# Local attention values in four row tiles of the transposed weights, constant products at the start, and a new order: attention and a two-layer product on one core

## The chip, the cores and the metric

The kernel runs on one core of a Trainium2 chip. The metric is the device time of one execution in microseconds (us). Five engines matter: TensorE (PE) multiplies matrices, VectorE (DVE), ScalarE (ACT) and GpSimd (POOL) work on elements, SyncE (SP) issues the transfers (DMA). Each engine takes its instructions in the order of its own list and waits on semaphores for the others.

## The reference

Eight batches of eight heads, 576 positions, 64 values per head. Two attentions are added: a global one on means of four positions, repeated four times, and a local one in which a position sees those less than four away. The sum, laid out as 4608 rows of 512, goes through a two-layer product with a squared ReLU.

```python
out_d = sm_attn(q_d, k_d, v_d)                     # on means of 4 positions: 144 x 144
out_up = np.repeat(out_d, factor, axis=2)
mask = np.abs(pos[:, None] - pos[None, :]) < factor
scores = scale * np.matmul(q, k.transpose(0, 1, 3, 2))
scores = np.where(mask, scores, -1000000000.0)
...
out_local = np.matmul(attn, v)
return (out_up + out_local).astype(np.float32)

h = x @ w_in                                       # 4608 x 512 by 512 x 2048
r = np.maximum(h, 0.0)
g = s * (r * r) + b
return (g @ w_out).astype(np.float32)
```

## The kernel before, in words

A unit is one batch and one pair of heads; there are 32, numbered 4 × batch + pair. The 128 partitions hold 2 heads × 64 values where a product runs over the values of a head.

Batches 0 to 2 (units 0 to 11) do the local attention on PE, in `banded`. A row of 576 positions is cut into 24 windows of 24 positions; a window needs 32 keys. `near` (tokens `l0` to `l11`) computes for each head the products of q and k window by window (tile sl, L416 to L421: a mask through a 16-bit product, then 24 small products in column tiles), takes the maximum and the difference on DVE (L431, L432), the exponential on ACT (L436), the sum and its reciprocal on DVE (L438 to L440), and normalises (L442), on POOL for batch 0 and on DVE for the others. DVE's 32×32 transpose (L449) turns the weights to keys × positions (tile pt). ACT then copies each of four 32-row blocks onto the diagonal of a 128×128 block for each group of four windows (tile db, L453); everything off the diagonal was set to zero at the start. A product of 128 rows of v (vw) with 96 columns of that block gives four windows at once (tile ol, L464), twice per unit, a half each, and DVE adds the half to the global part (ups) into x (L468). The global part of a unit is `far` (tokens `d0` to `d11`): `down` reduces q and k (L308, L310), multiplies (sa, L327), takes the softmax on DVE and ACT, transposes on PE, and multiplies with the means of v, which `values` (tokens `v0` to `v11`) adds up on POOL.

Batches 3 to 7 do the local part on POOL and DVE instead, in `local_unit` (tiles lqk, pr, st, pv, acc), and only the global part on PE. Their first block of q and k uses the buffer `big`, which before holds db of unit 0 as well.

Weights come as 64-bit numbers and are converted in 22 chunks (tokens `c0` to `c21`, `convert`): ACT L252, DVE L254 to L258, ACT L260, DVE L262. Both layers use pairs of high and low parts: three products each. `x` is split by `begin_x` and its like (xh on ACT, xl on DVE, L747). For a block t of 256 rows and an eighth p of the inner width the upper products are L617 (tile ph, token `G`, two for each t and p), ReLU, square and the high part are ACT's L630 to L632 (`R`), the low part is DVE's L637 (`V`), and the lower products are L691 to L693 (tile po, `H`). The row sums of the second weights, for the constant b, are added up on DVE (L650, L653, token `b`) and multiplied by ones on PE (cs, L658, token `s`); only then can the first blocks be written out (`evict`, L669).

What sets the order: for everything up to the 28th pair (t, p), the text PLAN. Each word is one step of the generator with that name; `wNi`, `wNo` and `qN` issue loads. `in_order` ties the instructions of PE, DVE, ACT and POOL to that order, engine by engine, and `tc.high_priority` puts all of it ahead of the rest. Behind it the code runs by `advance`, the same before and after.

Before the plan run the clears (L789 to L792): DVE sets dq and the blocks of unit 3 and unit 0 to zero, ACT copies zeros into those of units 1 and 2 (L218).

Of the kernel before, what the change touches and what calls it, by code (L numbers as in the profile page):

```python
# [11 lines left out]
F32 = mybir.dt.float32  # L12
F32R = mybir.dt.float32r
I32 = mybir.dt.int32
BF16 = mybir.dt.bfloat16
# [36 lines left out]
HF = 7  # L52
GROUPS = [(i // HP, i % HP // 2) for i in range(EU, B * HP, 2)]
# [33 lines left out]
def attention_ffn_kernel(ctx, tc, qk, vw_in, vr_in, vdm, qkn, vn, w_in, w_out, s_in, b_in, out):  # L87
# [65 lines left out]

    ident = cst.tile([P, P], F32, name="ident")
# [45 lines left out]
    db = one.tile([P, 2 * NG, P], F32, tag="big", name="db")  # L200

# [5 lines left out]
    diag = {0: (db, *blocks(dq, 0, dq[:, QV:]))}  # L207
# [3 lines left out]
    def clear(i):  # L211
        da, vm = room[i]["dg"], room[i]["sc"][:, 1536:1792]
        n = 2 * NG * P
        for part in (da[:, n : n + QV], vm, da[:, 0:n]):
            if i == 3:
                nc.vector.memset(part, 0.0)
            else:
                nc.scalar.copy(part, zero.to_broadcast([P, part.shape[1]]))  # L218
        diag[i] = (take(da, 0, [P, 2 * NG, P]), *blocks(da, n, vm))
# [66 lines left out]
    def add_values(b, hp, tmp, dg):  # L286

        _, _, vdr, vm = dg
# [685 lines left out]
```

## Time and profile before

| | us |
|---|---|
| median of 3 runs | 957.62 (956.99 to 958.03) |
| profiled execution | 957.84 |
| its span | 956.0 |

How to read the profile: times are those of one execution on the core. A row of a timeline has its start in the span, its length, the engine, the line, the operation, out<-in with their shapes, how many were merged, and in brackets how long the engine was idle before it and what ended that. A row of the stretches has the stretch, its length, then the busy time and count of PE, of PE's weight loads, of DVE, ACT and POOL, the granted clock of PE, the busy share of DMA and its rate. A row of waits says who waited for whom, how long in all, how often, and the longest. The records of fp32 products are two for each instruction.

The early part by slices of a fortieth of the span (23.9 us each); each digit is the busy share in tenths:

```profile
PE   6699999999999999999999999999999999999998
DVE  8999999845587788787868787887777321112021
ACT  7977774466552636344454544454544333333231
PEclk9699999999999999999999999999999999999999
```

### The profile page before, as it was taken

The numbers are of one execution on the slowest core, as the hardware profiler recorded it, in microseconds if no ns is written. First come the engines' busy times: TensorE is split into PE (matmuls) and PEld (weight loads), VectorE is DVE, ScalarE is ACT, GpSimd is POOL, SyncE is SP. The second block draws the span as 40 slices with busy tenths as digits, with TensorE's granted clock in tenths as the row PEclk, the third lists the DMA queues.
The fourth block names the chain that finished last, engine by engine and source line by source line (L and its number), as shares of the span: only waits on it lengthen the run. The fifth ranks groups of instructions, "written<-read, shape, count | busy, mean of one in ns | idle before, by whom it ended". The sixth has DMA issues, their size and how long they took to land.

```text
span 956.0 us, 18449 instructions
## 1 busy us (share of the span) xinstructions
PE 928.4 (97%) x7316; PEld 835.7 (87%) x7316; DVE 639.5 (67%) x1134; ACT 476.8 (50%) x1133; POOL 416.2 (44%) x440
## 2 busy tenths in 40 slices
PE   6699999999999999999999999999999999999998
PEld 5588888888898999998899999999899999999986
DVE  8999999845587788787868787887777321112021
ACT  7977774466552636344454544454544333333231
POOL 6401130010577676867776868676776200000000
PEclk9699999999999999999999999999999999999999
DMA  9755413123232323323232323232311000000000
GB/s 322 268 167 183 143 46 118 63 75 100 87 117 89 117 90 110 95 80 108 88 116 80 126 80 126 81 126 79 114 55 44 1 23 2 23 1 23 1 23 22
DMA packets 31750, 86.25 MB, mean 90 GB/s; under 512 B 3248, under 2 KB 7856, under 8 KB 31664
## 3 DMA queue, kind: packets, MB, share of 16 engines
q1 hardware_dynamic: 31664, 85.08, 26.9%
q8 instruction: 57, 0.93, 0.4%
q14 instruction: 29, 0.24, 0.1%
HBM read 75.63 MB, written 9.44 MB: 89 GB/s over the span
## 4 chain that ended last, share of the span: by engine, by line
PE 84%; DVE 7%; DMA 3%; POOL 2%; ACT 1%; issue 1%; SPq 0%; DVEq 0%; POOLq 0%
PE ph L617 38%; PE po L691 13%; PE po L692 13%; PE po L693 12%; PE sa L327 2%; PE ol L464 1%; PE up L368 1%; POOL pr L522 1%; DMA tqk<-in_qk_dram 1%; PE ot L554 1%; DMA wst<-in_moe_w_in_dram 1%; DMA tvd<-in_vdm_dram 1%; PE up L366 1%; PE sl L421 1%; DVE es L257 1%
## 5 line engine op out<-in xcount | busy, mean ns | idle before, releaser
L617 PE MATMUL ph<-xh,wi 128*128 128x256 f32 x2176 | 406.7, 280 | 1.5 <-DVE gl L637 1.5
L617 PEld LDWEIGHTS ph<-xh,wi 128*128 128x128 f32 x2176 | 342.0, 189 | 7.3 <-DVE gl L637 1.9
L617 PE MATMUL ph<-xl,wi 128*128 128x256 f32 x1152 | 323.4, 281 | 0.0
L522 POOL TENSOR_TENSOR pr<-lqk 128x576 f32<-128x576 f32 x140 | 201.3, 1461 | 77.7 <-DMA lqk<-in_qkn_dram 47.7
L617 PEld LDWEIGHTS ph<-xl,wi 128*128 128x128 f32 x1152 | 217.3, 189 | 4.5
L630 ACT ACTIVATE ph<-ph 128x512 f32<-128x512 f32 x144 | 83.7, 582 | 248.1 <-PE ph L617 239.4
L691 PE MATMUL po<-wo,gh 128*128 128x512 f32 x456 | 181.8, 399 | 2.0 <-DVE os L669 1.7
L693 PE MATMUL po<-wo,gl 128*128 128x512 f32 x456 | 179.1, 394 | 1.1 <-DVE gl L637 1.0
L692 PE MATMUL po<-wo,gh 128*128 128x512 f32 x456 | 180.2, 395 | 0.0
L637 DVE TENSOR_TENSOR gl<-ph,gh 128x512 fp32r<-128x512 f32 x114 | 77.9, 684 | 125.0 <-ACT gh L632 124.7
L544 POOL TENSOR_TENSOR acc<-acc,pv 128x576 f32<-128x576 f32 x80 | 121.0, 1512 | 48.8 <-DVE acc L544 25.9
L524 DVE TENSOR_REDUCE st<-pr 128x9 f32<-128x576 f32 x140 | 105.9, 757 | 31.7 <-POOL pr L522 28.2
L693 PEld LDWEIGHTS po<-wo,gl 128*128 128x128 f32 x456 | 85.7, 188 | 20.5 <-DVE gl L637 2.5
L691 PEld LDWEIGHTS po<-wo,gh 128*128 128x128 f32 x456 | 85.7, 188 | 18.7 <-DVE os L669 2.1
L632 ACT CAST gh<-ph 128x512 fp32r<-128x512 f32 x114 | 66.6, 586 | 66.4 <-PE po L692 61.1
L692 PEld LDWEIGHTS po<-wo,gh 128*128 128x128 f32 x456 | 85.8, 188 | 15.7 <-DVE wo L262 0.3
L297 POOL TENSOR_TENSOR dq<-vt 80x64 f32<-80x64 f32 x58 | 22.6, 401 | 174.5 <-PE up L368 172.9
L543 DVE TENSOR_TENSOR pv<-lv,st 128x576 f32<-128x576 f32 x120 | 86.9, 747 | 14.2 <-POOL acc L544 13.6
L631 ACT ACTIVATE ph<-ph 128x512 f32<-128x512 f32 x144 | 83.8, 583 | 3.5
L692 PE MATMUL po<-wo,gb 128*128 128x512 f32 x120 | 47.8, 398 | 0.0
L691 PE MATMUL po<-wo,gb 128*128 128x512 f32 x120 | 47.1, 392 | 0.0
L693 PE MATMUL po<-wo,gb 128*128 128x512 f32 x120 | 46.8, 392 | 0.0
(158 smaller groups left out, 1167.5 us busy)
## 6 DMA issues: line engine op xcount, KB each, us to landing
tqk<-in_qk_dram SPq DMA_DIRECT2D x30, 584.0 KB, 3.9
lqk<-in_qkn_dram SPq DMA_DIRECT2D x20, 768.0 KB, 4.6
lv<-in_vn_dram SPq DMA_DIRECT2D x20, 480.0 KB, 3.4
out_dram<-os SPq DMA_DIRECT2D x17, 512.0 KB, 3.0
wst<-in_moe_w_in_dram SPq DMA_DIRECT2D x7, 1024.0 KB, 6.2
wst<-in_moe_w_out_dram SPq DMA_DIRECT2D x7, 1024.0 KB, 5.0
tvd<-in_vdm_dram SPq DMA_DIRECT2D x29, 160.0 KB, 2.6
tvr<-in_vr_dram SPq DMA_DIRECT2D x29, 128.0 KB, 3.1
```

The source lines that it names most:

```text
L522: nc.gpsimd.tensor_tensor(pr, lqk[:, 0:CH], lqk[:, CH + o : 2 * CH + o], ALU.mult)
L524: nc.vector.tensor_reduce(ls[:, :, o], pr, AX.X, ALU.add)
L543: nc.vector.tensor_tensor(pv, lv[:, o : o + CH], w, ALU.mult)
L544: (nc.vector if o % 3 == 1 else nc.gpsimd).tensor_tensor(acc[:, :, h], acc[:, :, h], pv, ALU.add)
L617: nc.tensor.matmul(ph[:, j], wi[p][:, s, k, f], xk[:, k], start=k == 0 and s == 0 and xk is xh, stop=k == NK - 1 and s == 1)
L630: nc.scalar.activation(ph, ph, AF.Relu)
L631: nc.scalar.activation(ph, ph, AF.Square)
L632: nc.scalar.copy(gh, ph)
L637: nc.vector.tensor_tensor(gl, acc.pop((t, p)), gh.bitcast(F32), ALU.subtract)
L691: nc.tensor.matmul(po[m], gh[:, j, ms], wo[p][:, 0, j], start=first, stop=False)
L692: nc.tensor.matmul(po[m], gh[:, j, ms], wo[p][:, 1, j], start=False, stop=False)
L693: nc.tensor.matmul(po[m], gl[:, j, ms], wo[p][:, 0, j], start=False, stop=last)
```

## The change

**The local products.** The copies onto a diagonal go, and with them the tile db, its zeros and the part of the clears that made them. Each window is now a product of its own: 32 rows of v, by row tile of the window (tile position 32·w), with 24 columns of pt, into 64 partitions by head (column tile 64·h). A half f takes windows w = 2f and 2f + 1 of each group into two banks, ol0 and ol1, so a half is 24 products (before: 6) and two additions of 144 positions (before: one of 288), whose target is 6 pieces of 24 positions, 96 apart.

**Constant products.** DVE sets a 16-bit tile warm to one, and PE multiplies it with itself 14 times, 512 columns each, into a bank that nobody reads, ahead of q's first products.

**Normalising.** The multiplication runs on POOL for batches 0 and 1, on DVE for batch 2.

**The order.** PLAN is new throughout.

```diff
+WARM = 14
 PLAN = (
-    "d0 d0 l1 d1 l0 l1 d1 d2 d1 d3 d2 l1 d1 d3 d0 v1 l1 l0 l1 d1 l1 l0 d0 d1 l1 l2 d1 l0 d0 "
+    "d0 l0 d0 d1 l1 d0 l1 d1 l2 d0 d1 d2 d0 l0 d2 d1 l0 l2 d1 d2 l0 v2 l1 d3 d1 l2 l3 l2 d3 "
...
+    warm = two.tile([P, 4 * TB], BF16, tag="gh", name="warm")
+    nc.vector.memset(warm, 1.0)
+    spare = bank(7, [P, DM], "spare")
+    for _ in range(WARM):
+        nc.tensor.matmul(spare, warm[:, 0:P], warm[:, 0:DM], start=True, stop=True)
...
-    db = one.tile([P, 2 * NG, P], F32, tag="big", name="db")
...
-        n = 2 * NG * P
-        for part in (da[:, n : n + QV], vm, da[:, 0:n]):
+        for part in (da[:, 0:QV], vm):
...
-            (nc.vector if b else nc.gpsimd).tensor_tensor(
+            (nc.vector if b > 1 else nc.gpsimd).tensor_tensor(
...
-            for w in range(4):
-                ws = slice(32 * w, 32 * w + 32)
-                nc.scalar.copy(bd[ws, :, ws], pt[ws])
-            yield
...
             for f in range(2):
-                n = S // 2 // FAC
-                ol = banks([P, S // 2], "ol")
-                for gg in range(NG // 2):
-                    g = f * (NG // 2) + gg
-                    for h in range(2):
-                        hs = slice(64 * h, 64 * h + 64)
-                        pw = bd[:, h * NG + g, :].rearrange("p (w c) -> p w c", w=4)
-                        nc.tensor.matmul(
-                            ol[hs, 96 * gg : 96 * gg + 96], vw[:, g, hs], pw[:, :, 0:TW],
-                            start=True, stop=True)
+                ol = [banks([P, NG, TW], f"ol{i}") for i in range(2)]
+                for g in range(NG):
+                    for i in range(2):
+                        w = 2 * f + i
+                        ws = slice(32 * w, 32 * w + 32)
+                        for h in range(2):
+                            hs = slice(64 * h, 64 * h + 64)
+                            nc.tensor.matmul(
+                                ol[i][hs, g], vw[ws, g, hs], pt[ws, h * NG + g, 0:TW],
+                                start=True, stop=True, tile_position=(32 * w, 64 * h))
                 yield
-                nc.vector.tensor_tensor(
...
+                uv = ups.rearrange("p (g w s) -> p w g s", g=NG, w=4)
+                for i in range(2):
+                    w = 2 * f + i
+                    nc.vector.tensor_tensor(
+                        xv[:, w], ol[i].rearrange("p g (s j) -> p g s j", j=FAC),
+                        uv[:, w].unsqueeze(3).to_broadcast([P, NG, TW // FAC, FAC]), ALU.add)
...
-            nc.vector.memset(db, 0.0)
```

Lines behind the first edits shift by a few: what was L308, L421, L431, L442 and L449 is L311, L423, L433, L444 and L451 in the changed kernel; the new local products are L463, the new additions L470, the constant's memset and products L155 and L158. L617 to L693 keep their numbers.

Three places in the built order. First, DVE's start, before (dq and db are zeroed blocks, flat a buffer of units 1 to 3, tqk q and k of a unit, sl q's products):

```order
L216 MEMSET flat_80 128x416
L216 MEMSET flat_79 128x256
L216 MEMSET flat_80 128x1536
L792 MEMSET db_145 128x1536
L174 CAST idb_133<-ident_96 128x128
L308 TENSOR_REDUCE qd_200<-tqk_67 128x144
L310 TENSOR_REDUCE kd_201<-tqk_67 128x144
L176 CAST maskb_135<-mask_101 128x128
L177 CAST maskb_135<-mask_101 128x2x32
L308 TENSOR_REDUCE flat_69<-tqk_72 128x144
L310 TENSOR_REDUCE flat_69<-tqk_72 128x144
L431 TENSOR_REDUCE flat_71<-sl0_206 128x6
```

Both lists begin behind the memset of dq (L789), which stays. DVE's start in the changed kernel:

```order
L219 MEMSET flat_80 128x416
L219 MEMSET flat_79 128x256
L155 MEMSET warm_96 128x1024
L180 CAST idb_150<-ident_113 128x128
L311 TENSOR_REDUCE qd_212<-tqk_67 128x144
L313 TENSOR_REDUCE kd_213<-tqk_67 128x144
L182 CAST maskb_152<-mask_118 128x128
L183 CAST maskb_152<-mask_118 128x2x32
L311 TENSOR_REDUCE flat_69<-tqk_72 128x144
L313 TENSOR_REDUCE flat_69<-tqk_72 128x144
L433 TENSOR_REDUCE flat_71<-sl0_246 128x6
```

The two memsets of 1,536 are gone, the constant's stands in their place, and the first reduction of sl now reads the second of PE's sets (sl0_246) instead of the first.

Second, PE's start, before:

```order
L416 LDWEIGHTS idb_133
L416 MATMUL sl0_206<-maskb_135,idb_133 128x192
L421 MATMUL sl0_206<-tqk_72 32x32 x24
L416 LDWEIGHTS idb_133
L416 MATMUL sl0_234<-maskb_135,idb_133 128x192
L421 MATMUL sl0_234<-tqk_67 32x32 x24
L327 MATMUL sa_266<-flat_69,flat_70 96x144 x3
```

And in the changed kernel, from the last of the 14 constant products on:

```order
L158 LDWEIGHTS warm_96
L158 MATMUL spare_98<-warm_96 128x512
L418 LDWEIGHTS idb_150
L418 MATMUL sl0_216<-maskb_152,idb_150 128x192
L423 MATMUL sl0_216<-tqk_67 32x32 x24
L418 LDWEIGHTS idb_150
L418 MATMUL sl0_246<-maskb_152,idb_150 128x192
L423 MATMUL sl0_246<-tqk_72 32x32 x24
L330 MATMUL sa_275<-kd_213,dq_156 96x144 x3
```

The constant's products stand ahead of q's, and unit 0's set now comes before unit 1's.

Third, DVE at the weights of unit 4, the first of batch 1, before (pl are the weights, sm their sums, es, wi and wo weights of the two-layer product in conversion):

```order
L440 RECIPROCAL sm_818<-sm_818 128x12
L254 TENSOR_SCALAR es_869<-es_869 128x1024
L255 TENSOR_SCALAR es_869<-es_869 128x1024
L637 TENSOR_TENSOR gl_961<-ph_905,gh_960 128x512
L257 SCALAR_TENSOR_TENSOR es_822<-wst_159,es_822 128x512
L258 SCALAR_TENSOR_TENSOR es_822<-wst_159,es_822 128x512
L262 TENSOR_TENSOR wi_851<-es_853,wi_851 128x1024
L442 TENSOR_TENSOR pl_817<-pl_817,sm_818 128x384
L257 SCALAR_TENSOR_TENSOR es_869<-wst_665,es_869 128x1024
L258 SCALAR_TENSOR_TENSOR es_869<-wst_665,es_869 128x1024
L449 STREAM_TRANSPOSE pt_1091<-pl_817 128x384
```

And in the changed kernel:

```order
L442 RECIPROCAL sm_960<-sm_960 128x12
L260 SCALAR_TENSOR_TENSOR es_1077<-wst_175,es_1077 128x512
L261 SCALAR_TENSOR_TENSOR es_1077<-wst_175,es_1077 128x512
L451 STREAM_TRANSPOSE pt_1146<-pl_959 128x384
L433 TENSOR_REDUCE sm_1155<-sl0_1102 128x6
```

The multiplication between reciprocal and transpose has left DVE's list (it is L444 in POOL's now); two conversions of 512 stand between the two. Elsewhere in PE's list, 210 lower products (L691 to L693) stood ahead of the column sums L658 and 216 do now, while 456 upper products (L617) stand ahead of them in both. On the DMA queue the first block of the later batches (lqk) now comes ahead of batch 1's first q.

More of the change, by code (lines that the diff above doesn't have):

```diff
@@ L205, in blocks @@
                 take(vm, 0, [KM, 2, P]))
-    diag = {0: (db, *blocks(dq, 0, dq[:, QV:]))}
+    diag = {0: blocks(dq, 0, dq[:, QV:])}
     zero = dq[:, QV - 1 : QV]
@@ L218, in clear @@
                 nc.scalar.copy(part, zero.to_broadcast([P, part.shape[1]]))
-        diag[i] = (take(da, 0, [P, 2 * NG, P]), *blocks(da, n, vm))
+        diag[i] = blocks(da, 0, vm)
     wi, wo, wst = {}, {}, {}
@@ L286, in add_values @@
     def add_values(b, hp, tmp, dg):
-        _, _, vdr, vm = dg
+        _, vdr, vm = dg
         tvr, tvd = ld[(b, hp)]["vr"], ld[(b, hp)]["vd"]
@@ L300, in down @@
     def down(b, hp, banks, tmp, dg):
-        _, qc, vdr, vm = dg
+        qc, vdr, vm = dg
         tqk = ld[(b, hp)]["qk"]
@@ L396, in banded @@
         dg = diag[alt]
-        bd = dg[0]
         own = room[hp] if b == 0 and hp else None
@@ L450, in near @@
             yield
-            for w in range(4):
-                ws = slice(32 * w, 32 * w + 32)
-                nc.scalar.copy(bd[ws, :, ws], pt[ws])
-            yield
             vw = ld[(b, hp)]["vw"]
+            xv = x[:, hp].rearrange("p (g w s j) -> p w g s j", g=NG, w=4, j=FAC)
             for f in range(2):
-                n = S // 2 // FAC
-                ol = banks([P, S // 2], "ol")
-                for gg in range(NG // 2):
-                    g = f * (NG // 2) + gg
-                    for h in range(2):
-                        hs = slice(64 * h, 64 * h + 64)
-                        pw = bd[:, h * NG + g, :].rearrange("p (w c) -> p w c", w=4)
-                        nc.tensor.matmul(
-                            ol[hs, 96 * gg : 96 * gg + 96], vw[:, g, hs], pw[:, :, 0:TW],
-                            start=True, stop=True)
-                yield
-                nc.vector.tensor_tensor(
-                    x[:, hp, f * (S // 2) : (f + 1) * (S // 2)].rearrange(
-                        "p (s j) -> p s j", j=FAC),
-                    ol.rearrange("p (s j) -> p s j", j=FAC),
-                    ups[:, n * f : n * f + n].unsqueeze(2).to_broadcast([P, n, FAC]), ALU.add)
+                ol = [banks([P, NG, TW], f"ol{i}") for i in range(2)]
[8 more added lines that the diff above has]
+                                start=True, stop=True, tile_position=(32 * w, 64 * h))
+                yield
+                uv = ups.rearrange("p (g w s) -> p w g s", g=NG, w=4)
[4 more added lines that the diff above has]
+                        uv[:, w].unsqueeze(3).to_broadcast([P, NG, TW // FAC, FAC]), ALU.add)
                 if f == 1:
@@ L481, in first_unit @@
         part = banded(b, hp, banks)
-        for steps in ("ddv", "ddd", "ll", "ll", "lll", "ddd", "ddll", "dd", "ll", "ll"):
+        for steps in ("ddv", "ddd", "ll", "ll", "lll", "ddd", "ddl", "dd", "ll", "ll"):
             for which in steps:
@@ L791, in attention_ffn_kernel @@
                 clear(hp)
-            nc.vector.memset(db, 0.0)
     offset_mask()
-    at = {"sa": 0, "tp": 0, "up": 0, "tr": 1, "sl0": 1, "sl1": 0, "ol": 1}
+    at = {"sa": 0, "tp": 0, "up": 0, "tr": 1, "sl0": 1, "sl1": 0, "ol0": 0, "ol1": 1}
     def two_banks(*ids):
```

43 rows, old and new, of the table PLAN are left out of this document.

## The prediction

> **What bounds the kernel now.** I read the page first, then the table of stretches, then the waits of VectorE (DVE) and of TensorE (PE). The page says that PE is busy nearly all the time:
>
> ```profile
> span 956.0 us, 18449 instructions
> PE 928.4 (97%) x7316; PEld 835.7 (87%) x7316; DVE 639.5 (67%) x1134; ACT 476.8 (50%) x1133; POOL 416.2 (44%) x440
> ```
>
> A share of the whole span is an average over unlike stages, so the span is cut where the kernel changes its character: at the first reduction of q's products, at the last piece of x for the first matrix product, and at the column sums.
>
> ```profile
> 0.00:8.56 8.56, 1.19 (x50) 0.94 (x50) 6.93 (x13) 6.61 (x11) 6.50 (x24) 1.00 0.76 277
> 8.56:52.40 43.84, 34.75 (x583) 29.87 (x582) 42.31 (x95) 37.37 (x113) 20.69 (x36) 0.77 0.86 290
> 52.40:177.00 124.60, 121.44 (x1158) 106.19 (x1156) 117.67 (x185) 84.37 (x168) 14.16 (x24) 1.00 0.37 119
> 177.00:956.00 779.00, 770.99 (x5530) 698.68 (x5530) 472.60 (x845) 348.46 (x843) 374.81 (x356) 1.00 0.22 72
> ```
>
> The third busy column is DVE's: 42.31 of 43.84 and 117.67 of 124.60 before 177 us, then 472.60 of 779. PE (first column) has 770.99 of the last 779. So there are two stages. Up to the column sums DVE is full; behind them PE is. The waits say the same. These are DVE's own from 0 to 177 us, the longest beside the start:
>
> ```profile
> DVE sm L431 <- PE sl L421: 1.6, 2, 0.9
> DVE es L254 <- ACT es L252: 1.3, 2, 1.0
> ...
> DVE x L468 <- PE ol L464: 0.8, 1, 0.8
> DVE x L468 <- ACT gh L632: 0.7, 1, 0.7
> ```
>
> Together 4.4 us in 177. PE's from 49 us to the end:
>
> ```profile
> PE po L691 <- DVE os L669: 1.7, 1, 1.7
> PE ph L617 <- DVE gl L637: 1.5, 2, 1.2
> ...
> PE cs L658 <- DVE bias L653: 0.9, 1, 0.9
> ```
>
> PE's column sums (cs) wait 0.9 us for DVE's last addition to bias. That fixes how I count: **the column sums come when DVE has done all work ahead of them; the end comes when PE has done all work behind them.** By DVE's order that work is the same multiset of instructions before and after, but for the memsets, the x additions and four multiplications. Making ScalarE (ACT) or PE faster ahead of that point moves nothing unless DVE waited for it.
>
> **The change, term by term.** Times are of the profiled execution: 957.84 us, its span 956.0 and 1.84 around it. It lies 0.22 above the median shown, 957.62. About 0.2% (1.9 us) is what a measurement of this kernel can tell from no change.
>
> *Start.* DVE loses two long memsets, and the first reduction of sl has more to wait for.
>
> ```profile
> 2.55 1.34 DVE L216 MEMSET flat<- 128x1536 f32 x1 [0.27 <-issue]
> 4.15 1.34 DVE L792 MEMSET db<- 128x1536 f32 x1 [0.27 <-issue]
> 5.49 0.74 DVE L308 TENSOR_REDUCE qd<-tqk 128x144 f32<-128x576 f32 x1
> 7.24 0.75 DVE L308 TENSOR_REDUCE flat<-tqk 128x144 f32<-128x576 f32 x1
> 8.56 0.36 DVE L431 TENSOR_REDUCE flat<-sl 128x6 f32<-128x192 f32 x1
> ...
> 0.74 0.38 SPq L140 DMA_DIRECT2D tqk<-in_qk_dram  x1
> ...
> tqk<-in_qk_dram SPq DMA_DIRECT2D x1, 584.0 KB, 3.9
> ```
>
> The memsets took 3 us, but the first q lands only at 0.74 + 3.9 = 4.6, so its reduction comes at 4.6 instead of 5.49. From there to the second q's reduction are 7.24 − 5.49 = 1.75, and two reductions take 8.56 − 7.24 = 1.32: DVE stands before sl at about 7.7. Now PE. A memset of 1,024 elements at the rate of 1,536 in 1.34 takes 0.9, so the constant is ready at about 3.4 and 14 products of 512 columns start. What one of them takes:
>
> ```profile
> 49.53 0.41 PE L617 MATMUL ph<-xl,wi 128*128 128x256 f32 x1
> 49.74 0.63 PE L617 MATMUL ph<-xh,wi 128*128 128x256 f32 x2
> ...
> 178.10 0.39 PE L692 MATMUL po<-wo,gh 128*128 128x512 f32 x1
> 178.33 0.39 PE L693 MATMUL po<-wo,gl 128*128 128x512 f32 x1
> ```
>
> 256 columns at 49.5 us are 0.21 apart, thus 0.43 for 512 there; 512 columns later are 0.23 apart. So 14 take between 3.2 and 6.0; I take the middle, 4.6, to 8.0. Then come both heads' mask and q products, which the reduction needs:
>
> ```profile
> 7.38 0.32 PE L416 MATMUL sl<-maskb,idb 128*128 128x192 bf16 x1 [7.38 <-DVE maskb L177]
> 8.42 0.34 PE L416 MATMUL sl<-maskb,idb 128*128 128x192 bf16 x1
> ...
> 47.38 0.24 PE L416 MATMUL sl<-maskb,idb 128*128 128x192 bf16 x1 [2.21 <-DVE x L468]
> 47.55 0.62 PE L421 MATMUL sl<-tqk 64*32 64x32 f32 x48
> 48.11 1.41 PE L327 MATMUL sa<-kd,dq 128*96 128x144 f32 x6
> ```
>
> One such set took 1.04 at 7.4 us and 0.73 at 47.4. Two of the fast kind bring us to 8.0 + 1.5 + 0.1 = 9.6: **+1.0** against 8.56. Ends: all fast 3.4 + 3.2 + 1.5 + 0.1 = 8.2, −0.4; all slow 3.4 + 6.0 + 2.1 + 0.1 = 11.6, +3.0.
>
> The array's speed here is not taken from the granted clock: the profile calls it 1.00 to 8.56 us, and the set at 7.4 us, slower than the later one, contradicts that. The Trainium skill ("TensorE: Matmul & The Clock Gate", Part 1) says that the array starts at half rate and is released by about 3.4 us of activity. The spacings 1.04 and 0.73 agree. By an estimate from that page eight of the 14 would run slow, 3.4 + 6 × 0.23 = 4.8 us for all, and the term would be +1.2 instead of +1.0.
>
> *DVE's work behind it.* Rows that follow each other without a wait give the price of one:
>
> ```profile
> 17.64 0.36 DVE L432 TENSOR_TENSOR flat<-sl,flat 128x192 f32<-128x192 f32 x1
> 17.91 0.54 DVE L438 TENSOR_REDUCE sm<-pl 128x12 f32<-128x384 f32 x1
> ...
> 39.22 0.44 DVE L468 TENSOR_TENSOR x<-ol,ups 128x288 f32<-128x288 f32 x1
> 39.59 0.44 DVE L468 TENSOR_TENSOR x<-ol,flat 128x288 f32<-128x288 f32 x1
> ...
> 191.16 0.56 DVE L442 TENSOR_TENSOR pl<-pl,sm 128x384 f32<-128x384 f32 x1
> 191.76 0.58 DVE L449 STREAM_TRANSPOSE pt<-pl 128x384 f32<-128x384 f32 x1
> ```
>
> Four multiplications go to GpSimd (POOL): −4 × 0.60 = −2.4. DVE has other work for over a microsecond between the reciprocal and the transpose in each of these units, which covers POOL's 0.8. The x additions of eight units become 32 of 144 elements instead of 16 of 288. 288 cost 0.37, 192 cost 0.27, so 144 by the same slope 0.22: 32 × 0.22 − 16 × 0.37 = +1.1. No row writes the new strided pieces; between 0.18 (−0.2 in all) and the whole 0.37 (+5.9) I take 0.22, the nearest row's line. What POOL may hold up on DVE:
>
> ```profile
> 108.54 1.11 POOL L293 TENSOR_TENSOR vt<-tvd 80x256 f32<-80x256 f32 x1
> ...
> 109.10 1.11 DVE L255 TENSOR_SCALAR es<-es 128x1024 int32<-128x1024 int32 x1
> ...
> L255 DVE TENSOR_SCALAR es<-es 128x1024 int32<-128x1024 int32 x10 | 7.4, 736 | 0.3
> ```
>
> Beside a POOL addition this instruction took 1.11 against a mean of 0.74: +0.4. Four moved multiplications cost 0 to 1.6; I take +0.8. The term is −2.4 + 1.1 + 0.8 = **−0.5**.
>
> *Waits of DVE* are new throughout, for the plan is new: between all 4.4 gone and 4.4 more; I take **0**. The early ACT work (two clears, and four copies of the weights for each unit) vanishes ahead of the column sums, where DVE waited for ACT only 1.3 + 0.7: it counts within those ends. The first block of the later batches is now loaded ahead of batch 1's q, past which it moves on the DMA queue; DMA's busy share is 0.86 to 52 us, and what this delays counts within the same ends.
>
> *PE behind the column sums.* Counted in PE's order, 210 lower products (L691 to L693) stand ahead of them before, 216 after; the upper ones are equal. Six at 0.23 are done while PE had to wait anyway: **−1.4**.
>
> *The local products* of units 8 to 11 stand behind the column sums, eight halves.
>
> ```profile
> 126.54 0.72 PE L464 MATMUL ol<-db,tvw 128*64 128x96 f32 x12
> 127.18 0.51 PE L691 MATMUL po<-wo,gh 128*128 128x512 f32 x1
> ```
>
> A half took 0.64 for 12 records. Now it has 48. The nearest kind are q's 48, in two column tiles and narrow: 48.11 − 47.55 = 0.56, but with 32 columns of weights instead of 64. Ends per half 0.56 and 1.12; I take 0.64, no change: **0** (−0.6 to +3.8).
>
> Sum: +1.0 − 0.5 + 0 − 1.4 + 0 = −0.9, thus 956.9 against the profiled execution and **956.7** against the median: no change that can be told.
>
> **Rivals.** *The new plan closes DVE's remaining waits, and PE's later ones:* 4.4 from the row list, up to 3.2 for os and gl. For it: the ACT work that goes was in DVE's way once. Against: the old plan left little to close. With the 4.4 alone 952.3: faster.
>
> *The additions with scattered pieces cost what they cost whole,* 0.37 each: ahead of the column sums 32 × (0.37 − 0.22) = +4.8, thus 961.5: slower. It decides from 0.31 each (32 × 0.09 = 2.8, which turns −0.9 into +1.9). For it: fixed cost makes up much of a short one. Against: the line through 192 and 288.
>
> *A fixed price for each small product:* paced at half the speed of q's 48, a half takes the 1.12 from above, hence 8 × (1.12 − 0.64) = +3.8 and 960.5: slower. For it: four times the products for the same sums. Against it: q's 48 in 0.56 are 0.012 apart, narrow as they are. The Trainium skill's same page ("Wait — 56ns, not 53.3ns?") states a floor of about 25 ns from start to start however few columns; by an estimate from it a half would take 48 × 0.025 = 1.2 and the time would be 961.2, but q's rows here run below it.
>
> *DVE's waits double:* 961.1.
>
> *The change does not do what it says:* the constant's products leave the array slow, and the start ends at its +3.0: 958.7, within the bound, since DVE waited for PE 1.6 + 0.8 in all.
>
> **How the numbers follow.** Forecast 0.40 and the idle rival 0.02 make 0.42 for no change. Closed waits 0.34: faster. Dear additions 0.11, dear small products 0.05, doubled waits 0.08: slower, 0.24. The forecast's own range is 954.8 to 958.9. The one that I give reaches to the closed waits and to the slower rivals, 951.8 to 961.5, and leaves out what several terms would do together.
>
> **What would show it.** In the new profile the first reduction of sl at about 9.6; DVE over 94% busy to the column sums and these at about 177.5; additions of 144 elements 0.22 apart; a half of the local products in 0.64; 14 products in 4 to 5 us. A first x product well ahead of 49 us without a gain at the column sums would be the plainest sign that DVE sets the time. Column sums several microseconds before 177, or PE losing much less behind them, would make the forecast wrong.

## The result and the profile after

The changed kernel takes **970.00 us** (median of 6, 966.63 to 971.79) against 957.31 (median of 6, 955.93 to 958.04). The ratio is 1.0133 (1.0112 to 1.0154): slower by 12.7 us. The prediction said no change, with a range to 961.5.

The page of the changed kernel, to be read beside the lines of before:

```profile
span 967.2 us, 20153 instructions
PE 943.1 (98%) x8194; PEld 850.1 (88%) x8194; DVE 640.5 (66%) x1153; ACT 453.4 (47%) x1083; POOL 409.0 (42%) x444
...
DVE  6898999944578778877878788787877621211121
ACT  5665765354455454545454545454536333233231
```

DVE's busy time is what it was (639.5 before), ACT's is less by 23, PE's is more by 15. The column sums stand at 186.93 us instead of 176.94. Here are both kernels in the same four stretches, before first, then the changed one (columns as in the table of stretches above):

```profile
0.00:25.00 25.00, 15.81 (x428) 13.09 (x428) 22.42 (x49) 18.91 (x59) 17.60 (x45) 0.99 0.95 325
25.00:60.00 35.00, 27.36 (x295) 23.97 (x296) 34.21 (x71) 30.30 (x74) 9.59 (x16) 0.71 0.64 216
60.00:176.94 116.94, 114.15 (x1066) 99.88 (x1064) 110.21 (x172) 79.15 (x159) 14.16 (x24) 1.00 0.37 121
176.94:956.00 779.06, 771.05 (x5530) 698.74 (x5530) 472.66 (x845) 348.46 (x843) 374.81 (x356) 1.00 0.22 72
```

```profile
0.00:25.00 25.00, 16.25 (x436) 11.30 (x436) 16.91 (x40) 13.56 (x45) 12.01 (x38) 0.90 0.92 314
25.00:60.00 35.00, 29.41 (x572) 26.40 (x572) 30.59 (x72) 20.60 (x63) 11.03 (x21) 0.58 0.60 208
60.00:186.93 126.93, 121.07 (x1377) 107.39 (x1377) 119.41 (x191) 76.47 (x150) 20.37 (x30) 0.99 0.36 122
186.93:967.20 780.27, 776.34 (x5812) 705.03 (x5812) 473.58 (x853) 342.81 (x827) 365.62 (x356) 1.00 0.22 71
```

DVE's work up to the sums is 166.84 before and 166.91 after (three busy columns added). The time without work is 10.1 and 20.0: to 25 us 2.6 and 8.1, from 25 to 60 us 0.8 and 4.4, behind that 6.7 and 7.5. So the sums come 10.0 later because DVE stands 9.9 longer, 9.1 of it in the first 60 us. Behind the sums lie 1.2 more, which is less than two profiles of equal code differ by (see under the table of experiments). DVE's waits up to the sums say what for:

```profile
DVE flat L433 <- PE sl L423: 5.0, 3, 3.2
DVE x L470 <- PE ol L463: 4.2, 6, 1.5
DVE sm L433 <- PE sl L423: 2.5, 2, 2.3
```

11.7 us, all for PE: for q's products and for the local products. Before, these two were 1.6 and 0.8. What PE does there, in its timeline:

```profile
16.75 0.38 PE L423 MATMUL sl<-flat 64*32 64x32 f32 x23
20.55 0.55 PE L423 MATMUL sl<-flat 64*32 64x32 f32 x25 [3.42 <-issue]
...
42.91 1.49 PE L463 MATMUL ol<-pt,tvw 32*64 32x24 f32 x48
44.34 0.85 PE L369 MATMUL up<-flat 128*128 128x144 f32 x2
...
76.74 0.89 PE L463 MATMUL ol<-pt,tvw 32*64 32x24 f32 x48 [0.37 <-ACT ups L408]
77.56 0.38 PE L617 MATMUL ph<-xh,wi 128*128 128x256 f32 x1
```

PE stops for 3.4 us in the middle of a set, waiting for nothing that the profile shows. A half of the local products takes 44.34 − 42.91 = 1.43 at 43 us, where the granted clock is 0.50, and 0.82 at 77 us. The old half took 0.64 at full clock.

### The profile page after: what moved, and what is told of

It reads as the page before. It is cut to its first block, busy times and chain, and to the rows that moved or that the text cites. A ratio compares the mean times of both kernels' runs of the same rounds, so it can differ in the third digit from the quotient of the medians.

```text
span 967.2 us, 20153 instructions
## 1 busy us (share of the span) xinstructions
PE 943.1 (98%) x8194; PEld 850.1 (88%) x8194; DVE 640.5 (66%) x1153; ACT 453.4 (47%) x1083; POOL 409.0 (42%) x444
## 4 chain that ended last, share of the span: by engine, by line
PE 90%; DVE 6%; ACT 1%; issue 1%; POOL 1%; DMA 1%; DVEq 0%; SPq 0%; POOLq 0%
PE ph L617 40%; PE po L691 13%; PE po L692 13%; PE po L693 13%; PE sa L330 2%; PE ol L463 2%; PE up L371 2%; DVE bias L653 1%; PE sl L423 1%; PE ot L554 1%; PE up L369 1%; PE tr L358 1%; DVE es L260 1%; DVE es L261 1%; PE tp L356 1%
## 5 line engine op out<-in xcount | busy, mean ns | idle before, releaser
L617 PE MATMUL ph<-xh,wi 128*128 128x256 f32 x2176 | 411.6, 282 | 1.2 <-DVE gl L637 1.2
L617 PEld LDWEIGHTS ph<-xh,wi 128*128 128x128 f32 x2176 | 343.8, 190 | 6.4 <-DVE gl L637 1.4
L617 PE MATMUL ph<-xl,wi 128*128 128x256 f32 x1152 | 324.5, 282 | 0.0
L522 POOL TENSOR_TENSOR pr<-lqk 128x576 f32<-128x576 f32 x140 | 199.3, 1446 | 73.8 <-DMA lqk<-in_qkn_dram 52.6
L617 PEld LDWEIGHTS ph<-xl,wi 128*128 128x128 f32 x1152 | 217.9, 189 | 4.8
L691 PE MATMUL po<-wo,gh 128*128 128x512 f32 x456 | 183.0, 402 | 0.0
L693 PE MATMUL po<-wo,gl 128*128 128x512 f32 x456 | 179.0, 395 | 0.0
L544 POOL TENSOR_TENSOR acc<-acc,pv 128x576 f32<-128x576 f32 x80 | 114.6, 1433 | 56.6 <-DVE acc L544 33.7
L693 PEld LDWEIGHTS po<-wo,gl 128*128 128x128 f32 x456 | 85.9, 188 | 19.2
L691 PEld LDWEIGHTS po<-wo,gh 128*128 128x128 f32 x456 | 86.1, 189 | 15.5 <-issue 0.3
L300 POOL TENSOR_TENSOR dq<-vt 80x64 f32<-80x64 f32 x58 | 19.2, 339 | 115.5 <-PE up L371 114.2
L544 DVE TENSOR_TENSOR acc<-acc,pv 128x576 f32<-128x576 f32 x40 | 39.7, 992 | 11.8 <-POOL acc L544 11.8
L691 PE MATMUL po<-wo,gb 128*128 128x512 f32 x120 | 47.2, 393 | 0.0
L692 PE MATMUL po<-wo,gb 128*128 128x512 f32 x120 | 47.1, 392 | 0.0
```

The source lines that it names most:

```text
L522: nc.gpsimd.tensor_tensor(pr, lqk[:, 0:CH], lqk[:, CH + o : 2 * CH + o], ALU.mult)
L544: (nc.vector if o % 3 == 1 else nc.gpsimd).tensor_tensor(acc[:, :, h], acc[:, :, h], pv, ALU.add)
L617: nc.tensor.matmul(ph[:, j], wi[p][:, s, k, f], xk[:, k], start=k == 0 and s == 0 and xk is xh, stop=k == NK - 1 and s == 1)
L691: nc.tensor.matmul(po[m], gh[:, j, ms], wo[p][:, 0, j], start=first, stop=False)
L692: nc.tensor.matmul(po[m], gh[:, j, ms], wo[p][:, 1, j], start=False, stop=False)
L693: nc.tensor.matmul(po[m], gl[:, j, ms], wo[p][:, 0, j], start=False, stop=last)
```

## The experiments

Two theories stood first. **A**: the new order is the loss, since it leaves DVE with nothing but reductions of PE's sets while PE is late. **B**: the 24 narrow products per half are the loss. Theory E, that PE and no longer DVE paces the first stage of the changed kernel, came with the runs. In the table, the ratio is the 95% interval of a run's time to that of before, and the last two columns are microseconds: when the column sums come, and how long DVE stands without work to 25 us, from there to 60 us, and from there to the sums.

| run | edit | median us | ratio to before | sums at | DVE without work to 25 / to 60 / to the sums |
|---|---|---|---|---|---|
| before | | 957.31 | | 176.94 | 2.6 / 0.8 / 6.7 |
| changed | | 970.00 | 1.0112 to 1.0154 | 186.93 | 8.1 / 4.4 / 7.5 |
| e1 | before, new order | 974.86 | 1.0170 to 1.0200 | 192.32 | 6.8 / 8.9 / 7.1 |
| e2 | changed, no constant products | 969.63 | 1.0122 to 1.0156 | 187.10 | 9.2 / 4.7 / 7.6 |
| e3 | changed, 12 products per half | 963.12 | 1.0052 to 1.0095 | 182.39 | 10.7 / 1.4 / 4.0 |
| e4 | before, new products in batch 0 | 959.51 | 1.0018 to 1.0037 | 181.56 | 2.4 / 4.4 / 6.8 |
| e5 | changed, early wait filled | 969.35 | 1.0113 to 1.0142 | 187.42 | 7.7 / 5.1 / 8.9 |
| e6 | before, batch 1 normalised on POOL | 956.64 | 0.9984 to 1.0002 | 178.34 | 2.4 / 0.8 / 7.8 |
| e7 | changed, dense products added | 982.29 | 1.0241 to 1.0281 | 197.80 | 8.9 / 10.6 / 10.6 |
| e8 | changed, batch 1 normalised on DVE | 968.30 | 1.0096 to 1.0135 | 186.85 | 9.6 / 4.4 / 4.5 |
| e9 | changed, stop bridged | 971.93 | 1.0137 to 1.0176 | 189.37 | 9.0 / 4.8 / 8.8 |
| e10 | changed, 4 products per half | 961.50 | 1.0032 to 1.0064 | 181.73 | 10.2 / 1.1 / 4.2 |
| e11 | e10 and e5 | 960.64 | 1.0019 to 1.0044 | 183.24 | 9.5 / 1.1 / 7.0 |
| e12 | before, old products of batch 0 twice | 956.23 | 0.9984 to 1.0002 | 177.47 | 2.4 / 1.4 / 6.7 |
| e13 | changed, sums behind one more block | 971.90 | 1.0141 to 1.0174 | 189.58 | 8.6 / 4.4 / 9.2 |
| e14 | changed, old order at the start | 965.75 | 1.0078 to 1.0123 | 184.36 | 5.0 / 4.3 / 7.7 |
| e15 | e14 and e10 | 960.09 | 1.0025 to 1.0045 | 181.28 | 5.0 / 4.4 / 4.8 |

The sums and the time without work are those of one profiled execution each. One profile is not finer than about 2.5 us: behind the sums e4, e6 and e12, whose code there is that of before, took 776.5 us where the profile of before took 779.1.

**e1, the order alone.** The new PLAN in the kernel before, with the copies in the step of the transpose:

```diff
-    "d0 d0 l1 d1 l0 l1 d1 d2 d1 d3 d2 l1 d1 d3 d0 v1 l1 l0 l1 d1 l1 l0 d0 d1 l1 l2 d1 l0 d0 "
+    "d0 l0 d0 d1 l1 d0 l1 d1 l2 d0 d1 d2 d0 l0 d2 d1 l0 l2 d1 d2 l0 v2 l1 d3 d1 l2 l3 l2 d3 "
...
             nc.vector.transpose(pt, pl)
-            yield
             for w in range(4):
```

> The kernel before with the new PLAN alone: its block-diagonal copies, its products, its clears and its multiplications stay, and no constant products are added (the copies issue in the step of the transpose, since the new text has one step less there). Theory A (VectorE's order is the loss: the new text puts the second heads' reductions ahead of conversions and sums, and VectorE then stands while TensorE has no code behind its record 704 until about 20.5 us): VectorE idles over 15 us up to the column sums, these come after 183 us, and the time is 963 to 972. Theory B (the new local products are the loss, 48 narrow records for 12): the old products bring the old time back, 955 to 960, whatever the order.

It took 974.86, more than the changed kernel. That is above theory A's range too. Theory B alone is out: with the old products the new order is worse still. But it is no clean price of the order, since this order has no place for ACT's copies: DVE waited 3.8 us in one piece for ACT's part of a conversion, PE 3.8 for copies.

**e2, without the constant products.**

```diff
-    for _ in range(WARM):
-        nc.tensor.matmul(spare, warm[:, 0:P], warm[:, 0:DM], start=True, stop=True)
```

> The changed kernel without the 14 constant products and their memset. Theory A: TensorE stops behind the same record, the 704th, until 20 to 21.5 us, so what it did in the first 17 us is of no account: 967 to 972. Theory C (the constant products delay the start by the 0.95 us by which the first reduction of sl came later): 968 to 969.5, and no wait takes their place. Theory D (they are what keeps the array fast where it counts): over 973.

The memset of their tile goes with them. 969.63, no difference. PE came to the stop at 16.35 and went on at 20.58. The constant products do what they should (the clock's row goes to 1.00 at 6.5 us instead of 12.7) and it is of no use: behind the same record PE stands until about 20.5 either way.

**e3, e10: fewer products.** Each product takes two (e3) or all six (e10) groups with the weights of one, so that the other groups' values are wrong:

```diff
-                for g in range(NG):
+                for g in range(0, NG, 2):
...
-                                ol[i][hs, g], vw[ws, g, hs], pt[ws, h * NG + g, 0:TW],
+                                ol[i][hs, g : g + 2], vw[ws, g, hs], pt[ws, h * NG + g : h * NG + g + 2, 0:TW],
```

```diff
-                for g in range(NG):
+                for g in (0,):
...
-                                ol[i][hs, g], vw[ws, g, hs], pt[ws, h * NG + g, 0:TW],
+                                ol[i][hs], vw[ws, g, hs], pt[ws, h * NG : h * NG + NG, 0:TW],
```

> The changed kernel with half as many local products, twice as wide: one product takes two neighbouring windows with the weights of the first, so that the values of every second window are those of its neighbour's keys. Theory A: VectorE's stop at 17.9 to 21.2 us stays; its waits for the local products (4.2 us before the column sums) shrink below 2, and behind the sums eight halves lose 0.2 to 0.4 each: 963 to 968. Theory B: with the products' price halved most of the loss of 12.7 goes: 957 to 961.

> The changed kernel with 4 local products per half instead of 24, each 144 columns wide (all groups with the first group's weights, so that the local values are wrong but for a sixth). Theory E: by the spacing of 25.9 ns a record at the half clock eight early halves shrink from 1.43 to under 0.6 us, the later ones from 0.82 to under 0.5: TensorE gains some 6 us before the first x product is due and VectorE is the pace again, column sums at 178 to 182 us, 956 to 961. Rival (the new order alone costs most of the loss): column sums behind 183 us, over 962.

963.12 and 961.50: the number of products is worth 6.9 and 8.5 us, with the same columns written. DVE's time without work from 25 us on falls from 11.9 to 5.4 and 5.3. Here is e10 in the four stretches:

```profile
0.00:25.00 25.00, 17.17 (x402) 11.45 (x406) 14.79 (x35) 11.70 (x41) 10.67 (x36) 0.81 0.95 320
25.00:60.00 35.00, 26.91 (x311) 21.43 (x300) 33.95 (x80) 24.11 (x70) 12.79 (x22) 0.60 0.59 203
60.00:181.73 121.73, 115.62 (x1049) 100.07 (x1049) 117.50 (x188) 74.87 (x147) 22.05 (x30) 1.00 0.38 127
```

DVE has 33.95 of 35 from 25 to 60 us, close to the 34.21 of before, but 14.79 of the first 25. Theory B holds for the second stretch and not for the first. e3's time lies at the lower end of theory A's 963 to 968 and outside theory B's 957 to 961; DVE waited under 2 us for the products (0.8), as A had it. In e10 the sums are inside 178 to 182, the time is half a microsecond outside theory E's 956 to 961, and below its rival's 962; an early half by itself took 0.7 us, not under 0.6.

**e4, the new products in batch 0 with the old order.**

```diff
+            if b:
                 for w in range(4):
                     ws = slice(32 * w, 32 * w + 32)
                     nc.scalar.copy(bd[ws, :, ws], pt[ws])
...
+            if b == 0:
+                xv = x[:, hp].rearrange("p (g w s j) -> p w g s j", g=NG, w=4, j=FAC)
+                for f in range(2):
+                    ol = [banks([P, NG, TW], f"ol{i}") for i in range(2)]
...
```

> The kernel before, its PLAN as it was, with the new local products in batch 0 only (the copies of that batch go; the copies and products of batches 1 and 2 stay, and so do all clears). Theory A: the old order gives VectorE work while TensorE is late, so eight halves that take 1.4 instead of 1.0 us at the half clock hide: 955 to 959. Theory B: they are late for VectorE as in the changed kernel, 2.6 us and more by the waits before 56 us there: 960 to 964.

959.51, between the two ranges: the old order hides most, not all. The first 25 us are as before; the time that DVE loses without work is all in the second stretch (0.8 to 4.4). There PE runs at half clock to 57.7 us and stops once more inside the products:

```profile
41.48 3.23 PE L467 MATMUL ol<-flat 32*64 32x24 f32 x125
46.05 0.83 PE L467 MATMUL ol<-flat 32*64 32x24 f32 x19 [1.34 <-issue]
```

**e5, e8: DVE's side.** e5 moves unit 3's first difference behind work that is ready; e8 puts batch 1's normalising back on DVE:

```diff
-    "d2 v0 l2 d3 l3 d2 l1 l3 d1 d2 l2 d0 c0 d3 l2 d1 d2 c0 v1 l1 d1 d0 l3 l0 c1 l1 d2 c1 l1 "
+    "d2 v0 l2 d3 d2 l1 d1 d2 l2 d0 l3 l3 c0 d3 l2 d1 d2 c0 v1 l1 d1 d0 l3 l0 c1 l1 d2 c1 l1 "
```

```diff
-            (nc.vector if b > 1 else nc.gpsimd).tensor_tensor(
+            (nc.vector if b else nc.gpsimd).tensor_tensor(
```

> The changed kernel with one place of its PLAN altered: unit 3's first difference on VectorE (and its second set of products) stands behind unit 1's second difference, unit 1's reciprocal and unit 2's sum, whose inputs are there while TensorE stands behind record 704. Theory A (VectorE's idle time ahead of the column sums is the time): the wait of 3.24 us at 17.9 shrinks to about 1.4, the column sums come 1 to 2 us earlier, and the time is 968 to 969.2. Rival (TensorE sets the pace ahead of the sums too, it is late anyway): within 0.4 of the changed kernel's 970.

> The changed kernel with the normalising of batch 1 back on VectorE. Theory A (VectorE's waits leave room, but they lie before 60 and at 95 us, while these multiplications lie between): four multiplications of 0.60 lengthen VectorE's work by 2.4 us less what GpSimd had held up: column sums 1 to 2.5 us later, 971 to 972.5. Rival (TensorE is what is late there): within 0.5 of 970.

969.35 and 968.30. In e5 the long wait for sl shrank from 3.24 to at most 1.6, and the idle time came back at the next places where DVE needs PE; the sums came no earlier, and the time lies between the two ranges. In e8 DVE had 1.5 us more to do up to the sums (168.4 for 166.9), and they stayed too; the time is below both ranges, so nothing was lost. As one profile is no finer than 2.5 us, this rests on the times more than on the sums. By both, neither an early wait of DVE nor 1.5 us of its work sets the time in the changed kernel. Theory A's expectation of e5 and of e8 fell.

**e7, e9: PE's side.** e7 puts eight constant products of 144 columns ahead of each half in batch 0, e9 twelve of 512 columns ahead of the set in which PE stops:

```diff
+                for _ in range(4 if b == 0 else 0):
+                    for i in range(2):
+                        nc.tensor.matmul(
+                            ol[i], warm[:, 0:P], warm[:, 0 : NG * TW], start=True, stop=True)
                 for g in range(NG):
```

```diff
+                if (b, hp, h) == (0, 3, 0):
+                    wide = banks([P, DM], f"sl{h}")
+                    for _ in range(12):
+                        nc.tensor.matmul(
+                            wide, warm[:, 0:P], warm[:, 0:DM], start=True, stop=True)
+                    sl = take(wide, 0, [P, NG, 32])
```

> The changed kernel with eight more constant products of 144 columns ahead of each half of batch 0's local products, into the same banks, which the real ones then overwrite. Theory A1 (the narrow products leave the array's granted clock at half between 20 and 54 us): with dense products among them the clock's row goes back to 1.00 before 50 us and a half of the local products takes 0.8 us instead of 1.42, beside 0.5 to 1 us for the added ones; the time is within 3 of 970. Rival (the clock stays down for the gaps, whatever is multiplied): the row stays at 0.50 to 54 us and eight halves are each 1 us longer: 973 to 978.

> The changed kernel with 12 constant products of 512 columns ahead of unit 3's first set of products (into its bank, which the set then overwrites), so that TensorE works while its code behind record 704 is on the way. Theory E (TensorE paces the stage up to the first x product in the changed kernel, and the half clock from 20 to 54 us, which follows its stop, makes it late): the stop shrinks from 3.4 us to under 1.5, the granted clock stays 1.00 past 25 us, the first x product comes before 51 us, the column sums 2 to 5 us earlier, 964 to 968. Rival F (the clock falls at the next gap anyway, at 25 to 31 us): the clock's row is at 0.50 by 32 us and stays there, 968 to 972.

e7 took 982.29, above both ranges: eight times some 1.1 us of added products cost 12.3, that is all of it and more. PE paces this stage: theory E. The question about the clock went against A1: PE is busy all the time and the clock's row stays at 0.50:

```profile
35.00:55.00 20.00, 20.00 (x361) 18.16 (x360) 10.87 (x27) 6.62 (x17) 7.25 (x13) 0.50 0.23 78
```

In e9 the stop was gone and the clock stood at 1.00 from 20.0 to 26.8 us, then at 0.50 to 57.5, and the time was 971.93: rival F. Taking the stop away gains nothing by itself.

**e12, e6: the kernel before, tried from both sides.** Old products of batch 0 issued twice; batch 1's normalising on POOL.

```diff
+                        for _ in range(1 if b else 2):
                             nc.tensor.matmul(
                                 ol[hs, 96 * gg : 96 * gg + 96], vw[:, g, hs], pw[:, :, 0:TW],
```

```diff
-            (nc.vector if b else nc.gpsimd).tensor_tensor(
+            (nc.vector if b > 1 else nc.gpsimd).tensor_tensor(
```

> The kernel before with each of its local products in batch 0 issued twice, the second over the first: 96 more records of 96 columns in eight halves, by the spacings of 42 to 79 ns in that kernel 5 to 7 us more of TensorE before the first x product. Theory E (in the kernel before VectorE paces this stage, but TensorE's slack there is only its 3 to 4 us of waits behind 28 us): first x product 2 to 4 us later, the column sums 2 to 5 us later, 958.5 to 962. Rival (the old order hides it all): within 0.7 of before.

> The kernel before with the normalising of batch 1 on GpSimd, nothing else. Theory A (ahead of the column sums VectorE's work is the time in the kernel before): four multiplications of 0.60 less and up to 1.6 back from beside GpSimd: column sums 0.8 to 2.4 us earlier, 954.5 to 956.5. Rival: the transpose behind them waits for GpSimd, 957 to 959.

956.23 (e12) and 956.64 (e6), both no difference. e12 is nearest to its rival: twice the products in PE's early stage cost nothing, with the first x product at 49.42 (49.14 before). There are two reasons in its trace: PE had 2.2 us of waiting in front of that product, now gone, and the clock went to 1.00 at 40.1 and stayed there, so that 120 of the 192 records of these halves stood 42 ns apart instead of 80. e6 took four multiplications off DVE, and its work did not get less (167.4 for 166.85), because two kinds of conversions grew; its time lies between the two ranges, and its sums came no earlier (178.34). Here they are in e6 (line, shapes and count, busy time, mean ns of one, idle before); before had 7.4 us for L255 and 6.8 for L254 (means 736 and 675):

```profile
L255 DVE TENSOR_SCALAR es<-es 128x1024 int32<-128x1024 int32 x10 | 8.7, 870 | 0.3
L254 DVE TENSOR_SCALAR es<-es 128x1024 f32<-128x1024 f32 x10 | 7.6, 760 | 0.3 <-ACT es L252 0.3
```

**e11, e13, e14, e15: what is left with few products.** e11 is e10 with e5's place in PLAN. e13 moves DVE's last V ahead of the last additions to bias, and H ahead of the sums:

```diff
-    "c20 c20 G R b G c20 c21 V H c21 H b c21 b G R b c21 G c20 V H b b b H b b H R b b H b b "
-    "b V s H s E G E G d8 G d8 H R d8 l8 d8 G V d8 l8 G d9 R l8 d8 G d9 q10k d8 V d8 l8 H l8 "
+    "c20 c20 G R b G c20 c21 V H c21 H b c21 b G R b c21 G c20 V H b b b H b b H R b b H V b b "
+    "b H s s E G E G d8 G d8 H R d8 l8 d8 G V d8 l8 G d9 R l8 d8 G d9 q10k d8 V d8 l8 H l8 "
```

e14 begins PLAN with the 152 tokens that end with the split of the first x in before (one `l` less for each unit), and goes on with what the new PLAN has left; e15 is e14 with e10's products.

> The kernel with 4 wide local products per half (e10, wrong values for all groups but the first) and the altered place of PLAN (e5) together. Theory E (two paces lie side by side: TensorE's products, and the early order in which VectorE has only reductions of TensorE's sets to do; each hides what is won at the other): where the early wait shrank for nothing in e5, it now brings the column sums 1 to 2.5 us ahead of e10's 181.7 and the time to 958 to 960.5. Rival (the early waits are of no account even then): within 0.5 of e10's 961.5.

> The changed kernel with two tokens of its PLAN moved: VectorE's last subtraction (V) ahead of the last three additions to bias, and TensorE's lower products (H) that need it ahead of the column sums, so that TensorE has work where it stood for 2.1 us. Theory E (TensorE's order between the first x product and the sums loses time by waits, and each of them is in the end's time): 1 to 3 us less than the changed kernel, 967 to 969. Rival (VectorE sets the sums and nothing behind them can use the time): within 0.5 of 970.

> The changed kernel with the order of before for the first part (until the local products of batch 0 and the split of the first two blocks of x are issued) and its own order from there. Theory E2 (what is left with cheap products belongs to the order behind the first x product): the first x product at 52 to 56 us as in e4, and 131 to 136 us from there to the column sums as in the changed kernel (127 to 129 with the old order): 968 to 975. Rival G (it belongs to the order of the first 50 us, in which VectorE has only reductions to do): VectorE's idle time to 25 us falls from 8.1 to about 2.5, the column sums come at 181 to 184 us: 961 to 966.

> The order of before for the first part (e14) and 4 wide local products per half (e10, wrong values for all groups but the first) together. If the two causes are the whole loss and lie behind each other: 970.0 less 8.5 (e10) less 4.2 (e14), 956 to 958.5, the kernel before's time, with the column sums at 177 to 180 us. If they hide each other: 960 to 961.5, as e10 alone. If the later order holds a third cause of its own: over 961.5, or column sums behind 181 us.

e14 gains 4.2 (965.75), inside rival G's range though DVE's idle time to 25 us fell to 5.0 only, not 2.5, and the sums came at 184.36, just behind G's 184: the order of the first part is a cause of its own. Its interval and that of the changed kernel overlap by 0.001, so the size is less sure than that of e10. e13 gains nothing (971.90), against its expectation: the 2.1 us in which PE stands ahead of the sums are not won by this edit, and the sums come later (189.58). e11 (960.64) cannot be told from e10, and its sums came later, not earlier (183.24). And e15 (960.09) cannot be told from e10 either: the two causes hide each other. With both gone the time is still 1.0025 to 1.0045 times that of before, some 3.4 us more. At the seam of its two orders e15 has a wait of its own, 2.7 us of DVE for ACT's gh, so how much of this rest belongs to the later order stays open. The old order with the new products in all batches was not tried.

What part the half clock has is open too: it lasts past 52 us in every run with the new products, and no run took it away. One run of e2 speaks against it: its mean granted clock was 0.995 (2 × 0.005 × 967, some 10 us at half clock, where 0.980 makes some 39), and it took 969.97, no less than the 968.66 of a run at 0.980. It was not profiled.

None of these runs beats the kernel before by more than the measurement can tell.

## Why the prediction was wrong

The term that failed is **the waits of DVE**, which the prediction set to 0 between −4.4 and +4.4. By its own steps, against 11.2 us more of span (its bounds 958.9 and 951.8 have no working in it, but nothing hangs on them):

- *Start*: +1.0 forecast, +0.95 measured (first reduction of sl at 9.51 for 8.56), with 14 products in 4.5 us (3.41 to 7.93), close to the 4.6 chosen between 3.2 and 6.0. Right, but e2 shows that the whole edit is of no account.
- *DVE's work behind the start*: −0.5 forecast, +1.3 measured (161.2 to the sums for 159.9). The additions stood 0.22 apart as forecast:

```profile
41.08 0.52 DVE L470 TENSOR_TENSOR x<-ol,ups 128x144 f32<-128x144 f32 x2 [0.45 <-PE ol L463]
```

  Two in 0.52, one of 0.30, hence 0.22. All 32 were busy for 8.3 us instead of 7.1 for the 16, as forecast. What was mis-sized is the +0.8 for what the other instructions lose: they took some 2 us more. In the kernel before the move to POOL gives back all that it saves (e6); in the changed kernel it does not, since DVE's work grows by 1.5 us where the move is undone (e8). What else lengthened the others stays open. The Trainium skill ("SBUF — State Buffer", Who interferes with whom) says that a DVE instruction like L254 and L255 (a tensor_scalar) can contend with POOL in a two-port mode. The rows of e6 agree, 736 to 870 and 675 to 760 ns; in the changed kernel the same two take 695 and 710, one less and one more than before, so there it does not show.
- *Waits of DVE behind the start*: 0 forecast, **+7.7** measured (9.9 more without work, of which 2.2 lie in the start). The step that failed is the sentence that PE ahead of the sums moves nothing unless DVE waited for it. It was true of PE getting faster. Nothing was said of PE getting slower, and the local products were priced only behind the sums, eight halves of 24. The 16 ahead of them were not in the sum at all, though eight of these lie in the stretch whose mean clock the table gave as 0.77; they ran at 0.50, up to 1.42 us each. e7 (added products cost 12.3 us) and e8 (added DVE work costs nothing) show that the pace of this stage went from DVE to PE, e3 and e10 that the number of products made it so, e14 that the order of the start took 4.2 as well, and e15 that the two do not add up. Some 3.4 us have no cause shown.
- *PE behind the sums*: −1.4 forecast, with 0 for the products; +1.2 measured. By the spacing of 0.82 for 0.64 a half, eight halves cost 1.4 and up, inside the bounds given. The six products more stand ahead of the sums as forecast, and PE waits 2.1 there all the same. With some 2.5 us between profiles of equal code behind the sums, the two parts cannot be told apart.

Of the rivals, *DVE's waits double* named the place and missed the size, at a chance of 0.08; its price was a copy of the old waits and no mechanism. *A fixed price for each small product* was the right mechanism, charged at the wrong place: a record of 24 columns took 14.5 ns and one of 48 (e3) 15.1, so up to there a product costs by count; one of 144 (e10) took 27.6. The floor of 25 ns that the Trainium skill states ("TensorE: Matmul & The Clock Gate", "Wait — 56ns, not 53.3ns?") is not what the trace shows (14.5). The signs that the prediction named would have told it: DVE was to be over 94% busy up to the sums and had 166.91 of 186.93, 89%.

## What to carry to other kernels

An engine that is full up to a point is the pace only while the others keep their slack; where a change gives another engine four times the instructions, price them at the clock of that stage, ahead of the bound too, and ask how much slack they eat. Where two engines hand work to and fro, an early wait that is taken away comes back at the next handover (e5), and two causes do not add up (e15). Work taken off an engine that waits at that time is worth nothing: the memsets and the copies that went stood where, in the old order, nobody was held up for long.

## What was not expected of the hardware

- *Code on the way.* In every profile but e9's (where the added products cover it) PE stopped at the same place of its list, behind its 350th record of a product (the expectations call it record 704, with the loads of weights and the sequencer's entries), and went on at 20.5 to 22.9 us. In e2, without the 14 constant products ahead of it, it was the 350th again. In the stretch from 18 to 20 us the DMA engines of the changed kernel are full with loads, and one packet of another kind is among them:

```profile
q1 hardware_dynamic: 227, 0.78, 98.9%
q8 instruction: 1, 0.02, 3.5%
```

  Before had it too, but came there only at 20.98 us and stopped for 0.49. In all sixteen profiles PE goes on 1.2 to 1.6 us after the end of the second packet of this kind (16,384 bytes; in the changed kernel it ends at 19.32 and PE goes on at 20.55). Making PE faster at the start of this kernel runs into it. That the code is what is missing is inferred from these packets and from the fixed place, not tried by itself.
- *Two row tiles in alternation.* In unit 11 the built order put the 12 products of one row tile by themselves:

```profile
272.35 0.88 PE L463 MATMUL ol<-pt,tvw 32*64 32x24 f32 x24
273.16 0.39 PE L617 MATMUL ph<-xl,wi 128*128 128x256 f32 x1
```

  24 records took 0.81 us, as long as the 48 of two row tiles in turn at 76.74: 29.1 ns from start to start against 14.5. And e3's records of 48 columns stood 15.1 apart, so the columns cost next to nothing at this size. At the half clock the records of 24 columns in two row tiles stood 25.9 apart. The Trainium skill ("TensorEngine Tiling (Array Packing)", Instruction Overhead) says that a product of one column takes as long as one of 60; e3 agrees.
- *The half clock.* In the four profiles with the old products in batch 0 (before, e1, e6, e12) the row of the granted clock first leaves 0.50 for 1.00 behind 28 us at 38.6 to 41.7. In the thirteen with the new ones it does so only at 52.5 to 68.5, each time after the first x product. Being busy is not enough, as e7 shows: 20.00 of 20.00 us at 0.50. The Trainium skill ("TensorE: Matmul & The Clock Gate", Part 1) has one busy window of 3.4 us release the clock; that row of e7 disagrees, as far as the modelled ends of products can tell busy from idle. What counts as busy stays open.
- *The spread of the changed kernel* goes with the mean granted clock of its runs: 966.63 at 0.981, 969.00 and 969.44 at 0.978, 970.55 to 971.79 at 0.975.
